# Attention with decay and a two-layer FFN on one core: in the second sweep, the FFN's second layer by seven block products instead of eight

## The chip, the cores and the metric

The kernel runs on one core of one Trainium2 chip. The metric is the time of one execution in microseconds (us): the median of three runs is 1243.39 us, from 1242.62 to 1245.14. The engines are named as in the profile: PE multiplies matrices (PEld loads its weights), DVE, ACT and POOL do elementwise work, SP's queue issues the transfers. PSUM is the memory that PE writes, in eight banks of 128 x 512 fp32; SBUF is the memory that everything else works in.

## The reference, cut to what matters

```python
# q, k, v: (8, 8, 576, 64), f: (8, 8, 576); x: attention's output as (8, 576, 512)
def _moe_ref(x, U, V, w_ch1, w_ch2):
    xt = x.transpose(0, 2, 1)
    h = xt @ U @ V
    u = x + h.transpose(0, 2, 1)
    ch = np.maximum(u @ w_ch1, 0.0) @ w_ch2      # 512 -> 2048 -> 512
    return (u + ch).astype(np.float32)
```

Ahead of it stands a causal attention whose scores are shifted by cumulative sums of log f. The hidden layer has 2048 channels: 16 chunks of 128.

## The kernel before, in words

All is fp32. A matmul operand is held as two tiles, a high part (rounded for the matmul) and a low part (the rest), and a product is three matmuls: high by high, low by high, high by low.

**First sweep** (up to about 752 us). Batch by batch it computes attention, u, and the FFN over hidden chunks 0 to 5. It writes to DRAM u transposed, in two parts (`ud`), and u plus the FFN so far (`accd`). Near its end it decodes the weights of chunks 6 to 15, which arrive as 64-bit words, on DVE (`wb_unit`, with tile `xn2` as scratch).

**Second sweep** (line 950 to the end) computes chunks 6 to 15 for nine groups of 512 token rows: the main rows of the eight batches and one group of all their tails. `order` is batch 7, 0, 1, ..., 5, the tails, 6. I count groups from 1.

- Group 1 goes chunk by chunk: `first` (12 matmuls into a bank), `relu`, `second`.
- Groups 2 to 9 go by pairs of chunks, five to a group, in `pair_of_chunks`. The **first layer** of a pair is already done by Strassen's scheme (in Winograd's form): seven products M1 to M7, each of 6 matmuls of 256 columns (`product`, L1069). It needs sums of weight blocks (`weight_sums`, made once) and sums of token blocks: `token_sums`, eight POOL additions of 128 x 512 at the third pair of the group before (L1052 to L1057), and `token_part`, which splits the four sums into `Th` and `Tl` in the last pair. DVE adds the products up from PSUM, seven additions of 128 x 256 a pair (`plus`, L1092). ACT takes the ReLU (L970), and DVE makes the low part by SCALAR_TENSOR_TENSOR, STT from here on (L971), from SBUF alone.
- The **second layer** of a pair (`second`, L993) is 24 matmuls of 512 columns into four banks `O`, one for each 128 token rows, which collect over all five pairs. They are done one pair later, dealt out between the products (the list `ready`). After the fifth pair DVE adds each bank to the rows of `accd` (L997), and SP stores them (L999).

PE's order is the program's (`manual_schedule`); the other queues are ordered by the scheduler. The products of the first layer take turns in four banks, two of pool `psF` and two of `psX`. `load_u` (L962) brings both parts of the next group's tokens into one of two buffers, 2 MB a whole group ahead. `xn0` and `xn1` hold the rows of `accd` in turn, `xn2` the sums of tokens.

Of the kernel before, what the change touches and what calls it, by code (L numbers as in the profile page):

```python
# [40 lines left out]
def tile_decay_attention_moe(ctx, tc, qk, v, f, U, V, w1, w2, out):  # L41
# [917 lines left out]
    def load_u(g):  # L959
        t = up.tile([P, 2, NDC, MAIN], F32R, tag="u", name=f"u{g}")  # L960
        for x in range(2):
            nc.sync.dma_start(t.bitcast(F32)[:, x], ud[g, :, x])  # L962
# [4 lines left out]

    def relu(h, src, cols):
        hh, hl = h[0][:, cols], h[1][:, cols]
        nc.scalar.activation(hh, src, AF.Relu)  # L970
        nc.vector.scalar_tensor_tensor(hl, src, 0.0, hh.bitcast(F32), op0=ALU.max, op1=ALU.subtract)  # L971
# [12 lines left out]

    def second(z, i, h, x):

        k = z["done"][x]
        z["done"][x] += 1
        if k == 0:
            z["po"][x] = psO.tile([P, DM], F32, tag="O", name=f"O{z['g']}_{x}")  # L990
        po = z["po"][x]
        for m, (ht, wt_) in enumerate(((h[0], b2h), (h[1], b2h), (h[0], b2l))):
            nc.tensor.matmul(po, ht[:, P * x : P * x + P], wt_[i], start=k == 0 and m == 0, stop=k == NB - 1 and m == 2)  # L993
        if k < NB - 1:
            return
        g, o = z["g"], z["acc"][:, x]
        nc.vector.tensor_tensor(o, po, o, op=ALU.add)  # L997
        if g < B:
            nc.sync.dma_start(out[g, P * x : P * x + P], o)  # L999
# [9 lines left out]
    for i in range(NB // 2):  # L1009
# [9 lines left out]
    Th = sf.tile([P, 4, 2, HT], F32R, tag="uh", name="Th")  # L1019
    Tl = sf.tile([P, 4, 2, HT], F32R, tag="ul", name="Tl")  # L1020
    tmp = [sf2.tile([P, 2, HT], F32, tag="ost", name=f"sum{x}") for x in range(2)]
    tmp.append(sf.tile([P, 2, HT], F32, tag="TS", name="sum2"))
    tmp = [t[:, y] for t in tmp for y in range(2)]
# [21 lines left out]
    whole_u = xn[2][:, 0:4].rearrange("p q (c t) -> p q c t", c=2)  # L1045

    def token_sums(u):

        for q in range(4):
            c, t = 2 * (q // 2), HT * (q % 2)  # L1050
            h, l = (x[:, c : c + 2, t : t + HT].bitcast(F32) for x in u)
            nc.gpsimd.tensor_tensor(whole_u[:, q], h, l, op=ALU.add)  # L1052
# [8 lines left out]

    T1, T3, T4, T2 = ([x[:, q] for x in (Th, Tl)] for q in range(4))

    def product(bank, tag, name, a, b):
        ps = bank.tile([P, 512], F32, tag=tag, name=name)[:, 0:HT]
        m = 0
        for c in range(2):
            for x, y in ((0, 0), (1, 0), (0, 1)):
# [1 line left out]
                m += 1  # L1070
        return ps

    def pair_of_chunks(z, u, i, ready, renew):

        def go(k):
            for fn in ready[:k]:
                fn()
            del ready[:k]  # L1080
# [4 lines left out]
        def f(k, a, b):
            return product(psF, "F", f"M{k}_{g}_{i}", a, b)

        def x(k, a, b):
            return product(psX, "X", f"M{k}_{g}_{i}", a, b)

        def plus(dst, ps, other):
            nc.vector.tensor_tensor(dst, ps, other, op=ALU.add)  # L1092
# [7 lines left out]
        nc.scalar.copy(s1, m1)  # L1100
# [28 lines left out]

    order = [B - 1, *range(B - 2), B, B - 2]  # L1130
    u = cur
    ready = []
    with tc.manual_schedule(engines={ET.PE}):
        for n, g in enumerate(order):
            un = load_u(order[n + 1]) if n + 1 < NG else None
            acc = xn[(n + 1) % 2]
            if n:
                nc.sync.dma_start(acc[:, 0:NM], accd[g].rearrange("x p d -> p x d"))
            z = {"g": g, "acc": acc, "po": [None] * NM, "done": [0] * NM}
            if n == 0:  # L1140
                for i in range(NB):
                    h = first(g, u, i)
                    for fn in ready:
                        fn()
                    ready = [lambda z=z, x=x, i=i, h=h: second(z, i, h, x) for x in range(NM)]
                    if i % 2 and i < 6:
                        weight_sums(i // 2)
                    if i == NB - 3:
                        token_sums(un)
                for q in (3, 0, 1, 2):  # L1150
                    token_part(q)
            else:
                for i in range(NB // 2):
                    pair_of_chunks(z, u, i, ready, un and i == NB // 2 - 1)
                    if n == 1 and i < 2:
                        spare = xn[2].rearrange("p c d -> p (c d)")
                        weight_sums(3 + i, [spare[:, 256 * y : 256 * y + 256] for y in range(5)])
                    if i == 2 and un:
                        token_sums(un)
            u = un  # L1160
# [50 lines left out]
```

## Time and profile before

| | |
|---|---|
| median of three runs | 1243.39 us |
| the profiled execution: its time, its span | 1242.59 us, 1240.8 us |
| PE busy | 1204.0 us (97%) |
| DVE, ACT, POOL busy | 861.3, 645.5, 424.5 us |
| from 861.55 to 914.34 us (five pairs): PE, DVE, ACT, POOL busy | 52.79, 27.53, 12.42, 15.91 us |

The span runs from the first instruction to the last; the time has 1.8 us around it. A row of groups gives line, engine, operation, tiles, shapes and count, then busy time and the mean of one in ns, then the engine's idle time before them and who ended it. A matmul's duration includes its way through the array, so two that follow each other overlap: the pace of PE is read from starts. In the rows of a timeline, the first two numbers are start and duration in us, and the brackets at the end hold the idle time before and who ended it. PE's clock (PEclk) is a share of full speed.

### The profile page before, as it was taken

Reading aid. Unit: us, or ns where it says so; the run is one execution under the profiler, and the core shown is the slowest. Engines: PE = TensorE matmul, PEld = TensorE weight load, DVE = VectorE, ACT = ScalarE, POOL = GpSimd, SP = SyncE. Lnnn points to the kernel's source line nnn. Section 1 sums busy time; section 2 is a strip of 40 time slices with the busy share of each in tenths; the row PEclk is TensorE's granted clock in tenths of the full one; section 3 lists DMA queues with packets and bytes.
Section 4 is the critical chain, followed back from the end, with each engine's and each line's share of the span. In section 5 each row is a group of like instructions: output and inputs, shape, how many; then the busy total and the mean of one; then the engine's idle time right before and its main releaser. Section 6 shows DMA issues by size and latency. Waiting matters only on the chain.

```text
span 1240.8 us, 21851 instructions
## 1 busy us (share of the span) xinstructions
PE 1204.0 (97%) x7824; PEld 1066.0 (86%) x7824; DVE 861.3 (69%) x2195; ACT 645.5 (52%) x1741; POOL 424.5 (34%) x377
## 2 busy tenths in 40 slices
PE   8998999999999999999999999989999999999998
PEld 5776898998989988989989888878988889888897
DVE  8877778768778778787686799684554645546443
ACT  5777678767778758777675444322122221212211
POOL 4223454534544435454541000441341413315100
PEclk9999999999999999999999999999999999999999
DMA  6544344525335325425342345121120312213010
GB/s 183 153 132 130 79 105 111 151 68 159 95 89 164 88 78 148 117 71 171 79 125 76 120 141 229 34 69 69 68 102 35 136 43 95 85 52 137 1 35 35
DMA packets 67581, 125.87 MB, mean 101 GB/s; under 512 B 7408, under 2 KB 31984, under 8 KB 65424
## 3 DMA queue, kind: packets, MB, share of 16 engines
q1 hardware_dynamic: 67408, 124.47, 32.8%
q8 instruction: 62, 1.02, 0.3%
q14 instruction: 47, 0.39, 0.1%
q10 hardware_dynamic: 64, 0.00, 0.0%
HBM read 88.65 MB, written 35.78 MB: 100 GB/s over the span
## 4 chain that ended last, share of the span: by engine, by line
PE 82%; DVE 8%; ACT 6%; issue 2%; DMA 2%; SPq 0%; ACTq 0%; POOL 0%; DVEq 0%; POOLq 0%
PE O L993 20%; PE M L1069 16%; PE A L700 10%; PE B L718 9%; PE V L543 5%; PE T L440 3%; PE S L344 3%; PE Hb L979 2%; PE V L515 2%; PE S L345 2%; ACT P L373 1%; ACT G L309 1%; PE Tt L609 1%; PE St L344 1%; PE S L341 1%
## 5 line engine op out<-in xcount | busy, mean ns | idle before, releaser
L1092 DVE TENSOR_TENSOR sum<-M,sum 128x256 f32<-128x256 f32 x280 | 117.7, 422 | 173.3 <-PE M L1069 172.3
L970 ACT ACTIVATE bh<-sum 128x256 fp32r<-128x256 f32 x160 | 66.3, 418 | 256.9 <-DVE sum L1092 256.8
L373 ACT ACTIVATE P<-S,nm 128x128 f32<-128x128 f32 (+3 forms) x256 | 137.5, 539 | 57.5 <-DVE nm L365 48.3
L365 DVE CUSTOM_DVE_ANT_0 S<-S,mask 128x128 f32<-128x128 f32 (+3 forms) x256 | 125.7, 495 | 53.5 <-PE S L345 46.8
L993 PE MATMUL O<-b2h,bh 128*128 128x512 f32 x360 | 143.0, 397 | 0.0
L993 PE MATMUL O<-b2l,bh 128*128 128x512 f32 x360 | 142.4, 396 | 0.0
L993 PE MATMUL O<-b2h,bl 128*128 128x512 f32 x360 | 141.8, 394 | 0.0
L700 PE MATMUL A<-uh,w1h 128*128 128x256 f32 (+1 forms) x384 | 120.3, 313 | 1.8 <-DVE hl L704 1.7
L309 POOL CAST G<-qk 64x576 fp32r<-64x576 f32 x52 | 34.9, 671 | 250.1 <-PE St L345 149.5
L700 PE MATMUL A<-ul,w1h 128*128 128x256 f32 (+1 forms) x384 | 113.5, 296 | 0.0
L700 PE MATMUL A<-uh,w1l 128*128 128x256 f32 (+1 forms) x384 | 113.5, 296 | 0.0
L185 POOL TENSOR_TENSOR Tl<-xn,Th 128x512 fp32r<-128x512 f32 x32 | 41.3, 1303 | 201.7 <-PE M L1069 178.1
L971 DVE SCALAR_TENSOR_TENSOR bl<-sum,bh 128x256 fp32r<-128x256 f32 x160 | 92.4, 581 | 19.4 <-ACT bh L970 19.0
L1052 POOL TENSOR_TENSOR xn<-u 128x512 f32<-128x512 f32 x32 | 43.7, 1391 | 167.6 <-DVE b1l L71 106.4
L718 PE MATMUL B<-w2h,hh 128*128 128x512 f32 x216 | 90.4, 418 | 2.3 <-DVE hl L704 1.3
L440 PE MATMUL T<-ident,P 128*128 128x128 f32 x544 | 85.5, 273 | 0.0
L718 PE MATMUL B<-w2l,hh 128*128 128x512 f32 x216 | 85.1, 394 | 0.0
L718 PE MATMUL B<-w2h,hl 128*128 128x512 f32 x216 | 84.6, 392 | 0.0
L422 DVE TENSOR_TENSOR PTl<-T,PTh 128x512 fp32r<-128x512 f32 (+1 forms) x156 | 79.0, 524 | 6.6 <-ACT PTh L419 6.3
L993 PEld LDWEIGHTS O<-b2l,bh 128*128 128x128 f32 x360 | 67.7, 188 | 16.5
L322 POOL TENSOR_TENSOR G<-qk,G 64x576 fp32r<-64x576 f32 x52 | 74.4, 1431 | 15.6 <-ACT G L309 6.2
L993 PEld LDWEIGHTS O<-b2h,bl 128*128 128x128 f32 x360 | 68.2, 189 | 11.2
(240 smaller groups left out, 3543.7 us busy)
## 6 DMA issues: line engine op xcount, KB each, us to landing
qk<-in_qk_dram SPq DMA_DIRECT2D x104, 288.0 KB
u<-ud SPq DMA_DIRECT2D x16, 1024.0 KB
sr<-in_w_dram SPq DMA_DIRECT2D x20, 512.0 KB
vr<-in_v_dram SPq DMA_DIRECT2D x32, 256.0 KB
accd<-ost SPq DMA_DIRECT2D x32, 256.0 KB
xn<-accd SPq DMA_DIRECT2D x8, 1024.0 KB
out_dram<-xn SPq DMA_DIRECT2D x32, 256.0 KB
ud<-uh SPq DMA_DIRECT2D x7, 1024.0 KB
```

Source lines behind the costliest of these rows:

```text
L322: pin(el.tensor_tensor(g[oth, 2, cols], k[oth], gf[oth, 2, cols], op=ALU.subtract))
L365: nc.vector.tensor_tensor_reduce(ps[:, :w], ps[:, :w], mask[:, 512 - w : 512], scale=-SCALE, scalar=3.0e38, op0=ALU.add, op1=ALU.min, accu ...
L373: nc.scalar.activation(pt, ps[:, :w], AF.Exp, bias=z["nm"][:, col : col + 1], scale=-1.0, accum_out=z["sm"][:, col : col + 1])
L422: defer(2, lambda: nc.vector.tensor_tensor(dstl, src, dsth.bitcast(F32), op=ALU.subtract))
L440: nc.tensor.transpose(tp[:, P * x : P * x + P], z["P"][j][i][:, P * c : P * c + P], ident)
L700: nc.tensor.matmul(ps[:, :nt], wt[:, fc, c], ut[:, c, sl], start=m == 0, stop=m == 3 * NDC - 1)
L718: nc.tensor.matmul(ps, ht[:, fc, P * x : P * x + P], wt[:, fc], start=fc == 0 and m == 0, stop=fc == NA - 1 and m == 2,)
L970: nc.scalar.activation(hh, src, AF.Relu)
L971: nc.vector.scalar_tensor_tensor(hl, src, 0.0, hh.bitcast(F32), op0=ALU.max, op1=ALU.subtract)
L993: nc.tensor.matmul(po, ht[:, P * x : P * x + P], wt_[i], start=k == 0 and m == 0, stop=k == NB - 1 and m == 2)
L1069: nc.tensor.matmul(ps, a[x][:, c], b[y][:, c], start=m == 0, stop=m == 5)
L1092: nc.vector.tensor_tensor(dst, ps, other, op=ALU.add)
```

## The change

From group 3 on, the second layer of a pair is also done by Strassen's scheme. The pair's hidden block (256 channels x 512 tokens) is cut into four quarters and the weights likewise. Seven products N1 to N7, each of 6 matmuls of 256 columns, take the place of 24 matmuls of 512. In group 2 (`plain_products`) the second layer stays as it was, since its weight sums are made during that group.

- **Banks.** N1, N3, N4, N5 (`psM`) and N6, N7 (`psF`) each collect over the five pairs in a bank of their own. That leaves two banks (`psX`) for M1 to M7 and for N2, which is not collected in PSUM: DVE adds it to the output rows in each pair. Eight products a pair go through two banks in turn.
- **Hidden sums.** Three of the seven hidden operands are quarters after the ReLU (X11, X12, X22), as before. Four are sums of quarters (S1 to S4): a ReLU on ACT, four STTs on DVE, each of which needs the one before (L1243 to L1246), and four splits with the high part on ACT and the low part on POOL (L185). Before, the fourth quarter had its STT alone: three STTs more a pair on DVE, 20 to 35 a group.
- **End of a group.** Seven wide additions on DVE and one copy on ACT in place of four additions on DVE, and three additions on POOL (L1107), after which the rows are stored.
- **Weights.** `weight_sums2`: eight POOL, four DVE and four ACT instructions for each of five pairs, during group 1, group 2 and the start of group 3.
- **Tokens.** The buffers of `load_u` are gone. `load_direct` brings the three blocks that are used as they are, again for each group during its predecessor's last pair. `load_whole` brings the high part into `xn2` and the low part into that one of `xn0` and `xn1` that held the output of the group before. So the low part (1 MB) is loaded only when those rows have been stored.

The diff, cut to its core:

```diff
-    up = pool("up", 2)
-    hp_ = pool("hp", 4)
-    psO = ctx.enter_context(tc.tile_pool(name="psO", bufs=4, space=PSUM, reuse_waits="tile"))
+    two = pool("two")
+    psM = ctx.enter_context(tc.tile_pool(name="psM", bufs=1, space=PSUM, reuse_waits="tile"))
     psX = ctx.enter_context(tc.tile_pool(name="psX", bufs=2, space=PSUM, reuse_waits="tile"))
...
+    def load_whole(g, x, home):
+        nc.sync.dma_start(home[:, 0:NM], ud[g, :, x])
...
+    def weight_sums2(i):
+        eng = nc.gpsimd
...
+        whole(t0, 0, 1)
+        whole(t1, 0, 0)
+        whole(t2, 1, 1)
+        whole(t3, 1, 0)
+        nc.vector.tensor_tensor(t1, t0, t1, op=ALU.subtract)
...
+        for src, (h, l) in zip((t1, t0, t2, t3), [block2(i, 0, 1)] + SD[i]):
+            split(h, l, src, nc.scalar, eng)
...
-            nc.gpsimd.tensor_tensor(whole_u[:, q], h, l, op=ALU.add)
+            nc.gpsimd.tensor_tensor(whole_u[q], whole_u[q], low[:, c : c + 2, t : t + HT], op=ALU.add)
...
+        def ends_6():
+            add(u4, z["M"][6], u4)
+            add(u3, z["M"][7], u4)
+            add(u4, z["M"][5], u4)
+            for q in (2, 3):
+                add(quarter[q], u3, quarter[q], nc.gpsimd)
+            for x in (2, 3):
+                store(z["g"], acc, x)
+
+        def ends_3():
+            add(quarter[1], z["M"][3], quarter[1])
+            add(quarter[1], u4, quarter[1], nc.gpsimd)
+            for x in (0, 1):
+                store(z["g"], acc, x)
...
+        work = (
+            (1, X11, block2(i, 0, 0)), (4, X22, sd[2]), (2, X12, block2(i, 1, 0)), (7, S3, sd[0]),
+            (5, S1, block2(i, 0, 1)), (6, S2, sd[1]), (3, S4, block2(i, 1, 1)),
+        )
...
+        m3 = pr(3, W4, D3)
+        add(c12, m3, s4)
+        slot(3)
+        if plain:
+            relu(*S3, c12)
+            ready.extend(plain_products(z, i))
+            return
+        nc.scalar.activation(r21, c12, AF.Relu)
+        nc.vector.scalar_tensor_tensor(c22, c22, 0.0, r21, op0=ALU.max, op1=ALU.add)
+        nc.vector.scalar_tensor_tensor(r21, c11, 0.0, r21, op0=ALU.max, op1=ALU.subtract)
+        nc.vector.scalar_tensor_tensor(c11, c11, 0.0, c22, op0=ALU.max, op1=ALU.subtract)
+        nc.vector.scalar_tensor_tensor(c21, c21, 0.0, c11, op0=ALU.max, op1=ALU.add)
+        for src, (h, l) in ((r21, S3), (c22, S1), (c11, S2), (c21, S4)):
+            split(h, l, src, nc.scalar, nc.gpsimd)
+        ready.extend(output_products(z, i))
...
+                if i == 1 and nxt is not None:
+                    load_whole(nxt, 0, xn[2])
+                    load_whole(nxt, 1, other)
+                if i == 2 and nxt is not None:
+                    token_sums(other)
```

PE's order in a pair is now M1, N1, M6, N4, M5, N2, M2, N7, M7, N5, M4, N6, M3, N3, where the N belong to the pair before.

On DVE, before, at the border of the second and third pair of group 5 (batch 3; `M3_3_1` is M3 of batch 3, pair 1, counted from 0): the addition of M3, two STTs of which neither needs the other, and the additions of the next pair.

```order
L1092 TENSOR_TENSOR sum1_9781<-M3_3_1_11829,sum1_9781 128x256
L971 SCALAR_TENSOR_TENSOR bl3_3_11753<-sum1_9781,bh3_3_11752 128x256
L971 SCALAR_TENSOR_TENSOR bl3_2_11751<-sum1_9781,bh3_2_11750 128x256
L1092 TENSOR_TENSOR sum0_9780<-M6_3_2_11859,sum0_9780 128x256
L1092 TENSOR_TENSOR sum1_9781<-M5_3_2_11867,sum0_9780 128x256
L1092 TENSOR_TENSOR sum2_9782<-M2_3_2_11884,sum0_9780 128x256
```

At the same place now: `xn0`, `xn1` and `xn2` here are spare rows of those tiles that hold the temporaries, and `N2_3_1` is the product that is added to the output in SBUF.

```order
L1107 TENSOR_TENSOR xn0_105<-M3_3_1_12200,xn0_105 128x256
L1243 SCALAR_TENSOR_TENSOR xn1_106<-xn1_106 128x256
L1244 SCALAR_TENSOR_TENSOR xn1_106<-xn0_105,xn1_106 128x256
L1245 SCALAR_TENSOR_TENSOR xn0_105<-xn0_105,xn1_106 128x256
L1246 SCALAR_TENSOR_TENSOR xn2_107<-xn2_107,xn0_105 128x256
L1107 TENSOR_TENSOR sum2_9782<-M6_3_2_12244,sum2_9782 128x256
L1107 TENSOR_TENSOR xn0_105<-M5_3_2_12258,sum2_9782 128x256
L1107 TENSOR_TENSOR xn1_106<-N2_3_1_12266,xn1_106 128x2x256
L1107 TENSOR_TENSOR xn0_105<-M2_3_2_12274,sum2_9782 128x256
```

The chain of four STTs, behind a ReLU, now stands ahead of the addition that empties M6's bank, and the wide addition of N2 stands between those of M5 and M2.

On POOL, before, the whole work of a group (`u4` is the next batch's tokens):

```order
L1052 TENSOR_TENSOR xn2_107<-u4_11645 128x512 x4
L1054 TENSOR_TENSOR xn2_107<-xn2_107 128x512
L1055 TENSOR_TENSOR xn2_107<-xn2_107 128x512
L1056 TENSOR_TENSOR xn2_107<-xn2_107 128x512
L1057 TENSOR_TENSOR xn2_107<-xn2_107 128x512
L185 TENSOR_TENSOR Tl_9779<-xn2_107,Th_9778 128x512 x4
```

Now, from the end of a group to the token sums of the next but one: the three output additions, mixed with the four low parts of the first pair (`hb`, in the order S1, S3, S2, S4), then the token sums, mixed with those of the second pair.

```order
L1107 TENSOR_TENSOR xn0_105<-sum0_9780,xn0_105 128x2x256 x2
L185 TENSOR_TENSOR hb_9771<-xn1_106,hb_9771 128x256
L1107 TENSOR_TENSOR xn0_105<-sum1_9781,xn0_105 128x2x256
L185 TENSOR_TENSOR hb_9771<-xn1_106,hb_9771 128x256
L185 TENSOR_TENSOR hb_9771<-xn0_105,hb_9771 128x256
L185 TENSOR_TENSOR hb_9771<-sum2_9782,hb_9771 128x256
L1085 TENSOR_TENSOR xn2_107<-xn2_107,xn0_105 128x2x256 x3
L185 TENSOR_TENSOR hb_9771<-xn1_106,hb_9771 128x256
L1085 TENSOR_TENSOR xn2_107<-xn2_107,xn0_105 128x2x256
L185 TENSOR_TENSOR hb_9771<-xn1_106,hb_9771 128x256
```

S3 of the second pair, the last row, which N7 waits for, now stands behind all four L1085, and these read the low part of the tokens (`xn0`) that is loaded over the stored output.

More of the change, by code (lines that the diff above doesn't have):

```diff
@@ L980, in first, with store @@
                 m += 1
-        h = hidden(f"{g}_{i}")
-        relu(h, ps, slice(0, MAIN))
-        return h
[L985 to L997, printed above, removed]
+        flat = hb.rearrange("p k x t -> p (k x t)")[:, 2 * MAIN * (i % 3) : 2 * MAIN * (i % 3) + 2 * MAIN]
+        h = flat[:, 0:MAIN], flat[:, MAIN : 2 * MAIN]
+        relu(*h, ps)
+        return h
+    def store(g, acc, x):
+        o = acc[:, x]
         if g < B:
@@ L1002, in second @@
             nc.sync.dma_start(out[2 * x, MAIN:S], o[64:128])
+    def second(z, i, h, x):
+        if i == 0:
+            z["po"][x] = psM.tile([P, DM], F32, tag=BANKS[x], name=f"O{z['g']}_{x}")
+        po = z["po"][x]
+        for m, (ht, wt_) in enumerate(((h[0], b2h), (h[1], b2h), (h[0], b2l))):
+            nc.tensor.matmul(po, ht[:, P * x : P * x + P], wt_[i], start=i == 0 and m == 0, stop=i == NB - 1 and m == 2)
+        if i < NB - 1:
+            return
+        o = z["acc"][:, x]
+        nc.vector.tensor_tensor(o, po, o, op=ALU.add)
+        store(z["g"], z["acc"], x)
     n3 = 3 * 2 * P
@@ L1008, in tile_decay_attention_moe @@
     SW = []
-    for i in range(NB // 2):
+    for i in range(NK):
         blocks = []
@@ L1018, in tile_decay_attention_moe, with block2 @@
         SW.append(blocks)
[L1019 to L1023, printed above, removed]
+    wide = 4 * 2 * HT
+    turned = [sf.tile([P, wide + 2 * HD], F32R, tag=tag, name=name) for tag, name in (("uh", "Th"), ("ul", "Tl"))]
+    Th, Tl = (t[:, 0:wide].rearrange("p (q c t) -> p q c t", q=4, c=2) for t in turned)
+    places = [sw2[:, HD * y : HD * y + HD] for y in range(6 * NK - 4)]
+    places += [t[:, wide + HD * y : wide + HD * y + HD] for t in turned for y in range(2)]
+    SD = [[places[6 * i + 2 * x : 6 * i + 2 * x + 2] for x in range(3)] for i in range(NK)]
+    wides = [sf2.tile([P, 2 * HT], F32, tag="ost", name=f"sum{x}") for x in range(2)]
+    ends = sf.tile([P, 2 * HT], F32, tag="TS", name="sum2")
+    tmp = [t[:, HT * y : HT * y + HT] for t in [ends] + [x[:, NM] for x in xn] for y in range(2)]
     def block(i, r, c):
         return [w[2 * i + r][:, 2 * c : 2 * c + 2] for w in (b1h, b1l)]
+    def block2(i, r, c):
+        return [w[2 * i + r][:, HD * c : HD * c + HD] for w in (b2h, b2l)]
     def weight_sums(i, tmp=tmp):
@@ new lines, in plain_products, with one @@
+    def plain_products(z, i):
+        acc = z["acc"]
+        def one(x, r, h):
+            if i == 0 and r == x // 2:
+                z["M"][x] = psM.tile([P, DM], F32, tag=BANKS[x], name=f"O{z['g']}_{x}")
+            ps = z["M"][x]
+            for m, (p_, wt_) in enumerate(((0, b2h), (1, b2h), (0, b2l))):
+                nc.tensor.matmul(
+                    ps, h[p_][:, P * (x % 2) : P * (x % 2) + P], wt_[2 * i + r],
+                    start=i == 0 and r == x // 2 and m == 0, stop=i == NK - 1 and r != x // 2 and m == 2,
+                )
+            if i == NK - 1 and r != x // 2:
+                add(acc[:, x], ps, acc[:, x])
+                store(z["g"], acc, x)
+        work = [(x, r, h) for r, h, xs in ((0, X11, (0, 1)), (1, X22, (2, 3)), (1, X12, (0, 1)), (0, S3, (2, 3))) for x in xs]
+        return [lambda y=y: one(*y) for y in work]
@@ L1130, in tile_decay_attention_moe @@
     order = [B - 1, *range(B - 2), B, B - 2]
-    u = cur
+    turns = [0]
     ready = []
     with tc.manual_schedule(engines={ET.PE}):
[L1134 to L1160, printed above, removed]
@@ new lines, in tile_decay_attention_moe @@
+        z = {"g": order[0], "acc": xn[1], "po": [None] * NM}
+        load_whole(order[1], 0, xn[2])
+        load_whole(order[1], 1, xn[0])
+        for k in range(3):
+            load_direct(order[1], k)
+        for i in range(NB):
+            h = first(order[0], cur, i)
+            for fn in ready:
+                fn()
+            ready = [lambda z=z, x=x, i=i, h=h: second(z, i, h, x) for x in range(NM)]
+            if i % 2 and i < 6:
+                weight_sums(i // 2)
+            if i == NB - 4:
+                token_sums(xn[0])
```

187 lines of the change are left out of this document (125 added, 62 removed).

## Prediction

> **What bounds the kernel now.** I read the page first, then the table by stages, the chain of waits, and the timelines of single engines.
>
> ```profile
> PE 1204.0 (97%) x7824; PEld 1066.0 (86%) x7824; DVE 861.3 (69%) x2195; ACT 645.5 (52%) x1741; POOL 424.5 (34%) x377
> PE 82%; DVE 8%; ACT 6%; issue 2%; DMA 2%; SPq 0%; ACTq 0%; POOL 0%; DVEq 0%; POOLq 0%
> ```
>
> PE is busy for 97% of the span and carries 82% of the chain that ended last. In the part that changes it is more than that. The table by stages gives, for group 4 and for ten microseconds of group 2, PE, PEld, DVE, ACT and POOL busy, then the granted clock:
>
> ```profile
> 861.55:914.34 52.79, 52.79 (x331) 47.41 (x331) 27.53 (x60) 12.42 (x29) 15.91 (x13) 1.00 0.22 79
> 815.00:825.00 10.00, 7.41 (x41) 6.65 (x41) 9.94 (x27) 3.63 (x10) 1.29 (x1) 0.83 0.43 140
> ```
>
> From group 3 on PE never stops and has its full clock, and the others are half idle: whatever PE is spared counts in full, as long as nobody makes it wait. In group 2 it does wait, for DVE, which is full there (9.94 of 10.00).
>
> **PE's own work.** The chain gives PE's pace, and ACT's copy of M1, one per pair, the length of a pair.
>
> ```profile
> 1083.63 2.13 PE M L1069 x18
> 1106.86 2.11 PE O L993 x9
> 915.39 0.37 ACT L1100 COPY sum<-M 128x256 f32<-128x256 f32 x1 [1.29 <-PE M L1069]
> 925.94 0.38 ACT L1100 COPY sum<-M 128x256 f32<-128x256 f32 x1 [1.27 <-PE M L1069]
> ```
>
> A matmul of 256 columns takes 2.13/18 = 0.118 us, one of 512 takes 2.11/9 = 0.234. A pair now: 42 x 0.118 + 24 x 0.234 = 10.6; measured 52.79/5 = 10.56, and 10.55 between the copies. Afterwards it is 84 matmuls of 256 columns: 84 x 0.1183 = 9.94, and a product of six 0.71. Groups 3 to 9 have 35 pairs: 35 x 0.62 = **21.7 us less**. Group 2 keeps its matmuls.
>
> **DVE's chain.** What the new scheme asks of DVE is shown by these groups (count, then busy time and mean in ns): first a quiet stretch, then one in which POOL runs without a break. After them single instructions, and ACT's ReLU over the whole sweep.
>
> ```profile
> L1092 DVE TENSOR_TENSOR sum<-M,sum 128x256 f32<-128x256 f32 x8 | 3.4, 424 | 7.1 <-PE M L1069 7.1
> L971 DVE SCALAR_TENSOR_TENSOR bl<-sum,bh 128x256 fp32r<-128x256 f32 x4 | 1.7, 420 | 0.6 <-ACT bh L970 0.6
> ...
> L971 DVE SCALAR_TENSOR_TENSOR bl<-sum,bh 128x256 fp32r<-128x256 f32 x3 | 2.6, 872 | 0.0
> L1092 DVE TENSOR_TENSOR sum<-M,sum 128x256 f32<-128x256 f32 x3 | 1.2, 416 | 0.2 <-PE M L1069 0.2
> ...
> 924.14 1.27 DVE L971 SCALAR_TENSOR_TENSOR bl<-sum,bh 128x256 fp32r<-128x256 f32 x1
> 1000.34 0.28 PE L1069 MATMUL M<-Th,b1h 128*128 128x256 f32 x1
> 1000.61 0.42 DVE L1092 TENSOR_TENSOR sum<-M,sum 128x256 f32<-128x256 f32 x1 [1.54 <-PE M L1069]
> ...
> L970 ACT ACTIVATE bh<-sum 128x256 fp32r<-128x256 f32 x160 | 66.3, 418 | 256.9 <-DVE sum L1092 256.8
> ```
>
> An STT reads twice from SBUF: 0.42 us alone, 0.87 on average and up to 1.27 beside POOL. The sum, which reads PSUM once, stays at 0.42. It starts 0.27 after its product's end (the next product's first matmul starts at 1000.34). The Trainium skill, page "SBUF — State Buffer", section "Who interferes with whom", says that a DVE instruction with two SBUF inputs contends with a GpSimd (here POOL) instruction that reads SBUF, and one with a single SBUF input does not. On who contends the trace agrees; what that section says of how much is a rival, below.
>
> In a pair's order M3 ends at 13 x 0.71 = 9.24, that is 0.71 before the next pair. Counted from that pair's start: sum of M3 from -0.44 to -0.02, ReLU to 0.40, then four STTs each needing the one before, and only then the sum that empties M6's bank. N2 takes that bank and is due at 5 x 0.71 = 3.55. With 0.42 each the chain ends at 2.1 and the sum, held then by M6 itself, at 2.8: hidden. With 0.87 it ends at 3.9, the sum at 4.3: PE waits 0.75. With 1.27: 5.5, 5.9, PE waits 2.4. So the price of a chain hangs on what POOL does beside it.
>
> **POOL's queue at a group's start.** Its prices, over the sweep or an earlier stretch, with the load that the token sums wait for and the last stores:
>
> ```profile
> L1052 POOL TENSOR_TENSOR xn<-u 128x512 f32<-128x512 f32 x24 | 32.4, 1379 | 41.4 <-DMA u<-ud 41.4
> L185 POOL TENSOR_TENSOR Tl<-xn,Th 128x512 fp32r<-128x512 f32 x25 | 32.2, 1297 | 180.2 <-PE M L1069 159.6 <-ACT Th L182 20.6
> ...
> L185 POOL TENSOR_TENSOR VS<-vr,VS 128x640 fp32r<-128x640 f32 x26 | 40.7, 1566 | 25.8 <-ACT VS L182 24.0 <-DMA qk<-in_qk_dram 1.8
> L595 POOL TENSOR_TENSOR xl<-xn,xh 128x512 fp32r<-128x512 f32 x31 | 40.5, 1308 | 2.4
> ...
> 913.25 0.80 SPq L962 DMA_DIRECT2D u<-ud  x2
> 1235.81 2.43 SPq L999 DMA_DIRECT2D out_dram<-xn  x4
> ...
> 921.13 5.43 POOL L1052 TENSOR_TENSOR xn<-u 128x512 f32<-128x512 f32 x4 [6.67 <-DMA u<-ud]
> ...
> L997 DVE TENSOR_TENSOR xn<-O,xn 128x512 f32<-128x512 f32 x3 | 2.0, 682 | 0.3 <-PE O L993 0.3
> ```
>
> A low part of 256 columns isn't in the trace: half of 1.30 is 0.65; by 1308 against 1566 ns for 128 columns more it is 1308 - 2 x 258 = 0.79. I take 0.75. A store lands at most 1240.8 - (1235.81 + 2.43) = 2.6 after its issue; I take 2.0. Two MB took 921.13 - 913.25 = 7.9, so 1 MB 3.9 at least and 7.9 at most; I take 4.5, near the half.
>
> Now the low token part is loaded over rows that must first be added up and stored. From a group's start: M3 of its first pair ends at 9.24 with N6 before it, the sums of the end (0.27 + 0.42 + 0.68) carry to 10.65, two POOL additions to 13.25, S1 to 14.0, the third addition to 15.3. Store landed 17.4, low part landed 22.0. Then POOL does three L1085 to 26.0, S1 of the second pair to 26.75, the fourth L1085 to 28.1, S3 to 28.85. N7 in the third pair needs S3 and is due at 2 x 9.94 + 7 x 0.71 = 24.85. **PE waits 4.0.** With 1.0 for the store and 3.9 for the load it is 2.4; with a load of 7.9 it is over 7.
>
> POOL is in use until about 35.5, beyond the third pair's chain: 0.75 to 2.4 more, I take 1.5, the middle. Chains of the first pair (output additions) and the last (token parts) have POOL beside them for half their length: 0.45 each. That of the second pair falls into POOL's wait for the load, that of the fourth meets only its own low parts: nothing. Per group 4.0 + 1.5 + 0.9 = 6.4.
>
> - Groups 4 to 8: 5 x 6.4 = 32.
> - Group 3: its predecessor is stored by DVE's additions at the end of the first pair, so S3 is in time. 1.5 + 0.9 for the chains, and 1.6, between nothing and 2.4, for the last `weight_sums2` beside the first of them: 4.
> - Group 9 has no token work: 0.45 beside the output additions, and 0.5, between nothing and 0.75, for each of four chains beside low parts alone: 2.5.
>
> Together **+38.5**, from +10 (every chain hidden, N7's wait halved) to +55 (STTs at 1.27).
>
> **Group 2's start.** Rows of POOL, PE and ACT there:
>
> ```profile
> 794.50 2.92 POOL L1052 TENSOR_TENSOR xn<-u 128x512 f32<-128x512 f32 x2 [5.37 <-DVE b2l L71]
> ...
> 806.06 0.28 PE L1069 MATMUL M<-u,b1h 128*128 128x256 f32 x1
> ...
> 806.97 0.37 ACT L1100 COPY sum<-M 128x256 f32<-128x256 f32 x1 [1.02 <-PE M L1069]
> 815.91 0.37 ACT L1100 COPY sum<-M 128x256 f32<-128x256 f32 x1
> 830.85 0.37 ACT L1100 COPY sum<-M 128x256 f32<-128x256 f32 x1 [0.69 <-PE M L1069]
> ...
> 818.41 0.38 PE L1069 MATMUL M<-Th,swhh 128*128 128x256 f32 x1 [2.59 <-DVE sum L1092]
> ```
>
> Before, tokens lie in a buffer of their own; only the sum into `xn2` waits for the weights' decoding, whose scratch that is (794.50). Now the load of `xn2` itself waits for it: 794.5 + 4 = 798.5, four L1085 at 1.38 to 804, then four subtractions and, of the token parts, three, at 1.30 to 813.1. M6 needs the part `T2` and is due at 806.06 + 0.71 + 6 x 0.234 = 808.2: PE waits 4.9. If `weight_sums2` of pair 0, now in group 1, delays the decoding by 4, it is 9. Before, the second pair took 14.9 by the copies, 4.4 over 10.56, by its stall and the clock; `weight_sums` still fills DVE, now behind a first wait, and I let it cost 5.5: 4.9 + 5.5 - 4.4 = **+6**, from +3 (half of it falls together with the new wait) to +12.
>
> The rest of group 2 gets four `weight_sums2`: 32 POOL instructions of 0.75, 16 STT-like ones on DVE with two SBUF inputs (0.42 to 1.27, 7 to 20 us) beside sums that PE waits for: **+4**, from 0 to +8.
>
> **The end.** The last matmuls and DVE's additions behind them:
>
> ```profile
> 1230.15 7.02 PE O L993 x30
> 1235.09 2.79 DVE L997 TENSOR_TENSOR xn<-O,xn 128x512 f32<-128x512 f32 x4 [3.57 <-PE O L993]
> ```
>
> After the last pair, 30 matmuls of 7.02 become 42 of 256 columns, 4.97: that is in the 0.62. But from M3's end on, S1's STT ends at 1.95, its high part at 2.4, its low part at 3.1, S3's at 3.9, and N7 is due behind N3, N1, N4 and N2, at 2.84: a wait of 1.0. And behind the last DVE addition POOL's (1.30) now stands ahead of the store: **+2.3**, from 1 to 3.5.
>
> **The sum.** The profiled execution took 1242.6 (span 1240.8 and 1.8 around it), near the median, 1243.4. -21.7 + 38.5 + 6 + 4 + 2.3 = +29.1: **1272**.
>
> **The rivals.**
>
> - *The waits are hidden.* A store of 1.0, a load of 3.9, four L1085 at 1.30 (-0.3) and low parts of 0.65 (-0.2): N7 waits 2.0; every chain hides: -21.7 + 10 + 4 + 1 + 2 = -4.7, about 1238. For it: DVE has 27.53 of 52.79 in use, and seven products of cover per chain. Against it: S3 is behind four L1085 in POOL's queue whatever its speed. It decides once N7's wait and the chains together come to less than (21.7 - 7)/5 = 2.9 a group instead of 6.4. Chance 0.22.
> - *The gain is just eaten:* N7 waits 2.4 and the chains take 0.1 a group; 12.5, and 9 elsewhere, against 21.7: no change. Chance 0.06.
> - *STTs at 1.27 throughout and the clock falls.* N7 4.0, the clock behind it 1.7, the third pair's chain 2.4, two half-covered ones 0.55 each: 9.2 a group; 5 x 9.2 + 6 + 3 = 55, group 2 +10 and +6, end +3: -21.7 + 74 = +52, about 1295. For it: POOL's work doubles, from 15.91 to 20 x 0.75 + 12 x 1.3 + 3 x 1.3 = 34.5 a group. In 815 to 825 a wait of 2.59 stood beside a clock of 0.83, that is 10 x 0.17 = 1.7 lost; N7's wait is longer. Against: the mean beside POOL was 0.87. Chance 0.22. The Trainium skill, page "TensorE: Matmul & The Clock Gate", section "Why this matters for your kernels", warns of idle gaps of PE over some 3 us; the row with 2.59 agrees roughly.
> - *DVE and POOL exclude each other.* An STT would wait for a whole POOL instruction, 1.30 + 0.42 = 1.72: third pair's chain at 7.3, PE waits 4.2 instead of 1.5, in six groups +16: 1288. Against: 1.27 is the longest shown. Chance 0.05. The Trainium skill, page "SBUF — State Buffer", section "Who interferes with whom", calls the shared pair of ports an exclusive lock, by which 1.72 would be seen; the 1.27 speaks against it.
>
> That the change does something else can be left out: PE's order has the 84 matmuls.
>
> **How the numbers follow.** Forecast 1272 (own range 1255 to 1287): 0.45. A measurement can tell some 0.2% (2.5 us). Faster 0.22, same 0.06, slower 0.45 + 0.22 + 0.05 = 0.72. The range takes in most of the first and third rival: 1236 to 1297.
>
> **What would show it.** Copies of M1 9.94 apart in undisturbed pairs; in the third pair of groups 4 to 8 a wait of PE of about 4 ahead of N7, released by POOL; waits of 1 to 2 ahead of N2, released by DVE; M6 of group 2 held about 5. I am wrong if N7 waits under 2, or if chains beside POOL stay near 0.42 an STT.

## The result and the profile after

The changed kernel takes 1295.08 us (median of four runs, 1292.88 to 1295.25) against 1243.97: a ratio of 1.0407, 95% interval 1.0389 to 1.0425. The direction held: slower was forecast. The time lies in the wide range, 1236 to 1297, which takes in most of two rivals, but outside the forecast's own, 1255 to 1287: 29 us were forecast and 51 measured. From the page of the profile after, PE's line and the chain:

```profile
PE 1209.7 (94%) x8454; PEld 1098.5 (85%) x8454; DVE 974.7 (75%) x2376; ACT 708.7 (55%) x1908; POOL 593.3 (46%) x578
PE 64%; DVE 15%; ACT 7%; POOL 6%; issue 4%; DMA 4%; POOLq 0%; SPq 0%; ACTq 0%; DVEq 0%
```

PE's share of the chain fell from 82% to 64%; DVE, POOL and DMA took it over. Where the time went is read from the copies of M1, whose distance is the length of a pair. First those at which groups 3 and 9 begin, of the kernel before, then of the changed one:

```profile
862.56 0.37 ACT L1100 COPY sum<-M 128x256 f32<-128x256 f32 x1 [1.29 <-PE M L1069]
1179.52 0.37 ACT L1100 COPY sum<-M 128x256 f32<-128x256 f32 x1 [1.29 <-PE M L1069]
```

```profile
874.67 0.35 ACT L1214 COPY sum<-M 128x256 f32<-128x256 f32 x1
...
1046.81 0.36 ACT L1214 COPY sum<-M 128x256 f32<-128x256 f32 x1
1057.81 0.37 ACT L1214 COPY sum<-M 128x256 f32<-128x256 f32 x1 [0.27 <-PE M L1102]
1069.53 0.37 ACT L1214 COPY sum<-M 128x256 f32<-128x256 f32 x1 [0.49 <-PE M L1102]
1084.61 0.37 ACT L1214 COPY sum<-M 128x256 f32<-128x256 f32 x1 [0.49 <-PE M L1102]
1094.64 0.37 ACT L1214 COPY sum<-M 128x256 f32<-128x256 f32 x1 [0.49 <-PE M L1102]
1105.01 0.35 ACT L1214 COPY sum<-M 128x256 f32<-128x256 f32 x1
...
1224.25 0.35 ACT L1214 COPY sum<-M 128x256 f32<-128x256 f32 x1
```

Up to group 3 the change loses 874.67 - 862.56 = 12.1 us. Groups 3 to 8 take 349.6 instead of 317.0, 32.6 more; group 9 and the end, with spans of 1291.1 and 1240.8, 66.9 instead of 61.3, 5.6 more: 50.3 in all.

The rows from 1046.81 to 1105.01 are group 6. Its pairs take 11.00, 11.72, 15.08, 10.03 and 10.37, where the matmuls alone take 9.94. PE's own rows in that group show who held it (the number before the arrow is PE's idle time):

```profile
1050.15 0.51 PE L1125 MATMUL N<-b2h,hb 128*128 128x256 f32 x2 [0.86 <-DVE xn L1107]
1061.09 0.50 PE L1125 MATMUL N<-b2h,hb 128*128 128x256 f32 x2 [0.46 <-DVE sum L1107]
...
1063.63 0.62 PE L1125 MATMUL N<-sw,hb 128*128 128x256 f32 x3 [0.59 <-POOL hb L185]
...
1077.20 0.86 PE L1125 MATMUL N<-sw,hb 128*128 128x256 f32 x5 [3.23 <-POOL hb L185]
```

The first two are N2, waiting for DVE in the first and second pair; the other two are N7, waiting for S3's low part, in the second pair and, for 3.23, in the third. What POOL did before that, and the low part's load on SP:

```profile
1070.79 3.78 POOL L1085 TENSOR_TENSOR xn<-xn,xn 128x512 f32<-128x512 f32 x3 [5.81 <-DMA xn<-ud]
1074.52 0.72 POOL L185 TENSOR_TENSOR hb<-xn,hb 128x256 fp32r<-128x256 f32 x1
1075.20 1.26 POOL L1085 TENSOR_TENSOR xn<-xn,xn 128x512 f32<-128x512 f32 x1
1076.42 1.42 POOL L185 TENSOR_TENSOR hb<-xn,hb 128x256 fp32r<-128x256 f32 x2
...
1065.49 0.33 SPq L972 DMA_DIRECT2D xn<-ud  x1
```

POOL idles 5.81 for the load (issued 1065.49, used 1070.79), then adds three blocks, S1's low part, the fourth block, and only then S3's. That is the chain that the prediction wrote out. What its sum did not count stands in the table of group 6 by stages (PE, PEld, DVE, ACT, POOL busy, granted clock):

```profile
1046.81:1105.01 58.20, 53.05 (x422) 51.95 (x422) 40.91 (x82) 20.18 (x51) 34.83 (x35) 0.97 0.29 100
1073.00:1077.20 4.20, 0.97 (x9) 0.76 (x8) 0.69 (x1) 0.00 (x0) 4.20 (x6) 1.00 0.00 0
1077.20:1084.00 6.80, 6.80 (x44) 6.80 (x45) 4.20 (x8) 1.54 (x4) 6.57 (x6) 0.75 0.42 154
```

Behind the wait PE runs for 6.80 us at 0.75 of its clock: 1.7 lost again.

### The profile page after: what moved, and what is told of

The parts are those of the page before. It is cut to its first block, busy times and chain, and to the rows that moved or that the text cites. A ratio compares the mean times of both kernels' runs of the same rounds, so it can differ in the third digit from the quotient of the medians.

```text
span 1291.1 us, 24113 instructions
## 1 busy us (share of the span) xinstructions
PE 1209.7 (94%) x8454; PEld 1098.5 (85%) x8454; DVE 974.7 (75%) x2376; ACT 708.7 (55%) x1908; POOL 593.3 (46%) x578
## 4 chain that ended last, share of the span: by engine, by line
PE 64%; DVE 15%; ACT 7%; POOL 6%; issue 4%; DMA 4%; POOLq 0%; SPq 0%; ACTq 0%; DVEq 0%
PE A L700 9%; PE B L718 9%; PE M L1102 9%; PE N L1125 9%; PE V L543 5%; PE T L440 3%; PE S L344 2%; POOL xn L1085 2%; PE V L515 2%; PE S L345 2%; DVE xn L1107 2%; DVE hb L976 2%; POOL hb L185 2%; DMA xn<-ud 2%; PE S L341 1%
## 5 line engine op out<-in xcount | busy, mean ns | idle before, releaser
L185 POOL TENSOR_TENSOR hb<-xn,hb 128x256 fp32r<-128x256 f32 x122 | 95.4, 806 | 95.3 <-ACT hb L182 95.3
L975 ACT ACTIVATE hb<-xn 128x256 fp32r<-128x256 f32 x105 | 43.9, 418 | 168.4 <-DVE xn L1107 168.4
L1125 PE MATMUL N<-b2h,hb 128*128 128x256 f32 x560 | 110.3, 289 | 11.4 <-DVE sum L1107 7.0
L1125 PE MATMUL N<-sw,hb 128*128 128x256 f32 x546 | 86.4, 292 | 21.9 <-POOL hb L185 21.9
L1125 PEld LDWEIGHTS N<-b2h,hb 128*128 128x128 f32 x560 | 87.9, 193 | 14.7 <-DVE sum L1107 8.6
L1125 PEld LDWEIGHTS N<-sw,hb 128*128 128x128 f32 x546 | 75.5, 198 | 24.5 <-POOL hb L185 24.4
L976 DVE SCALAR_TENSOR_TENSOR hb<-xn,hb 128x256 fp32r<-128x256 f32 x105 | 65.3, 631 | 26.2 <-ACT hb L975 26.2
L1085 POOL TENSOR_TENSOR xn<-xn,xn 128x512 f32<-128x512 f32 x32 | 41.7, 1328 | 89.2 <-DMA xn<-ud 89.2
L322 POOL TENSOR_TENSOR G<-qk,G 64x576 fp32r<-64x576 f32 x52 | 74.6, 1434 | 15.6 <-ACT G L309 6.2
L1125 PE MATMUL N<-b2l,hb 128*128 128x256 f32 x280 | 80.2, 286 | 0.0
L323 POOL TENSOR_TENSOR G<-qk,G 64x576 fp32r<-64x576 f32 x52 | 74.9, 1441 | 5.1 <-ACT G L309 4.9
```

The costliest lines, as they stand in the source:

```text
L185: leng.tensor_tensor(dl, src, dh.bitcast(F32), op=ALU.subtract)
L322: pin(el.tensor_tensor(g[oth, 2, cols], k[oth], gf[oth, 2, cols], op=ALU.subtract))
L323: pin(em.tensor_tensor(g[own, 1, cols], q[own], gf[own, 0, cols], op=ALU.subtract))
L976: nc.vector.scalar_tensor_tensor(l, src, 0.0, h.bitcast(F32), op0=ALU.max, op1=ALU.subtract)
L1125: nc.tensor.matmul(ps[:, y], a[p_][:, P * y : P * y + P], w[q_], start=(i == 0 or k == 2) and y == 0 and m == 0, stop=(i == NK - 1 or k == ...
```

## The experiments

The theory: POOL's queue holds S3 behind token sums that wait for the load, and the clock falls behind that wait. The rival: POOL simply has too much to do, and where it runs, DVE's chain of STTs is slow.

### e1: no load for POOL to wait for

```diff
                     load_whole(nxt, 0, xn[2])
-                    load_whole(nxt, 1, other)
```

> The load of the low token part is left out from group 2 on (the token sums add the old rows in its place), so that POOL no longer waits for store and load; its work is the same. Now the third pairs of groups 4 to 8 take 14.1 to 16.7 us instead of 9.94, 28 in sum. Theory (N7's wait on S3, behind token sums that wait for the load, and the lower clock behind that wait): all five come down to about 10, the time to 1267. Rival (POOL has too much work, and beside it DVE's chain is too slow): the token sums now stand beside the chains of the first two pairs, most of the 28 comes back there, 1280 or more.

Measured: 1285.70, ratio 1.0322 (1.0303 to 1.0340). The copies of group 6:

```profile
1048.60 0.36 ACT L1214 COPY sum<-M 128x256 f32<-128x256 f32 x1
1059.60 0.37 ACT L1214 COPY sum<-M 128x256 f32<-128x256 f32 x1 [0.27 <-PE M L1102]
1074.36 0.35 ACT L1214 COPY sum<-M 128x256 f32<-128x256 f32 x1
1084.67 0.37 ACT L1214 COPY sum<-M 128x256 f32<-128x256 f32 x1 [0.48 <-PE M L1102]
...
1068.57 0.42 DVE L1107 TENSOR_TENSOR xn<-M,sum 128x256 f32<-128x256 f32 x1 [3.20 <-POOL hb L185]
...
1066.65 0.86 PE L1125 MATMUL N<-sw,hb 128*128 128x256 f32 x5 [1.27 <-POOL hb L185]
```

The third pair is down from 15.08 to 10.31, so the load was what held it. But the second is up from 11.72 to 14.76: the token sums now mix with the first pair's low parts. PE waits 1.27 for S3's low part (the last row) and, in pieces of up to 0.5, for DVE, which itself waits 3.20 for a low part before it may overwrite its source. The theory's mechanism held, its number (1267) did not; the rival's number did.

### e2: POOL in the order of the program

```diff
-    with tc.manual_schedule(engines={ET.PE}):
+    with tc.manual_schedule(engines={ET.PE, ET.Pool}):
```

> POOL works in the order of the program: the token sums behind the low parts of the second pair and the third, all else of the change as it is; load and store stay. Theory: S3 of the second pair no longer waits for the load, third pairs of groups 4 to 8 at 10 to 11; the third output addition now stands ahead of S1 and S3 of the first pair, up to 1 more in each second pair; 1267 to 1273. Rival (POOL's amount of work, not its order): token sums run beside the third and fourth chain and Tl comes late, 1285 or more.

Measured: 1289.25, ratio 1.0350 (1.0334 to 1.0367). By the copies of M1, third pairs came to 10.1, but the last pairs of a group rose from 10.4 to between 14.0 and 15.6. PE, DVE and POOL at the start of such a last pair, in group 4:

```profile
981.24 0.80 PE L1125 MATMUL N<-b2h,hb 128*128 128x256 f32 x2 [2.94 <-DVE xn L1107]
...
976.63 1.40 DVE L1244 SCALAR_TENSOR_TENSOR xn<-xn,xn 128x256 f32<-128x256 f32 x1
978.07 1.38 DVE L1245 SCALAR_TENSOR_TENSOR xn<-xn,xn 128x256 f32<-128x256 f32 x1
979.48 1.37 DVE L1246 SCALAR_TENSOR_TENSOR sum<-sum,xn 128x256 f32<-128x256 f32 x1
980.77 0.41 DVE L1107 TENSOR_TENSOR xn<-M,sum 128x256 f32<-128x256 f32 x1
...
976.39 1.36 POOL L1088 TENSOR_TENSOR xn<-xn 128x512 f32<-128x512 f32 x1
977.83 1.33 POOL L1089 TENSOR_TENSOR xn<-xn 128x512 f32<-128x512 f32 x1
979.24 1.33 POOL L1090 TENSOR_TENSOR xn<-xn 128x512 f32<-128x512 f32 x1
...
981.20:987.00 5.80, 5.76 (x27) 5.77 (x28) 1.78 (x4) 1.63 (x4) 4.78 (x6) 0.50 0.30 97
```

The chain fell beside the last token sums. Each STT lasts as long as the POOL addition beside it, 1.4 instead of 0.42; the sum of M6 comes late, N2 waits 2.94, and the clock stands at 0.50 for 5.8 us (the last row, by stages). Again one wait was exchanged for another, and again the rival seemed to win.

### e3: everything but the products of the second layer

```diff
-pair_of_chunks(z, i, ready, renew if nxt is not None and i == NK - 1 else None, n == 1)
+pair_of_chunks(z, i, ready, renew if nxt is not None and i == NK - 1 else None, True)
```

From group 3 on it multiplies by weight blocks that `weight_sums2` has overwritten; the work is that of the plain products.

> All groups use plain_products: no chain, no hidden sums, no products N, 24 matmuls of 512 columns a pair as before; buffers, two banks for M1 to M7, loads and weight sums of the change stay. Theory (chain and N7 make the waits): groups 3 to 9 take 52.8 each again, only the 12 us of group 1 and 2 stay, 1256. Rival (two banks in place of four and the low load over the stored rows cost by themselves): groups 4 to 8 stay at 55 or more, 1270.

Measured: 1259.33, ratio 1.0113 (1.0095 to 1.0132). By the copies of M1, groups 3 to 8 take 52.2 to 52.9, as before the change. Two banks, the new loads and their order cost nothing as long as no chain and no N7 hang on them: what remains is the start of the sweep.

### e4: the wait on N7 filled with matmuls by zero

```diff
+            if k == 7 and i == 1 and 3 <= z["n"] <= 7:
+                for _ in range(26):
+                    nc.tensor.matmul(ps[:, 0], zero, w[0], start=False, stop=False)
```

> In the third pair of groups 4 to 8, 26 matmuls by a tile of zeros stand ahead of N7, 26 x 0.118 = 3.1 us, in N7's own bank; they fill the wait of 3.2 to 4.5. Theory (a gap of PE of that length is followed by a lower clock, which costs 1.4 to 2.9 again): the wait stays, the clock stays full behind it, 5 x 2 = 10 less, about 1285. Rival (the clock falls for another reason, or matmuls by zero do not count): 1295, or up to 10 more where N7 was ready earlier.

Measured: 1288.49, ratio 1.0352 (1.0329 to 1.0374). The filling in group 6, and the stage behind it:

```profile
1070.10 3.27 PE L1127 MATMUL N<-sw,zero 128*128 128x256 f32 x26
...
1074.00:1080.10 6.10, 6.10 (x54) 6.10 (x53) 4.33 (x8) 1.55 (x4) 5.87 (x6) 1.00 0.54 173
```

N7 starts no earlier, but the clock stays at 1.00 where it was 0.75. By the copies, the third pairs of groups 4 to 8 took 14.10, 16.09, 15.08, 16.72 and 16.15 and now 14.17, 14.18, 14.19, 14.33 and 14.18: 7.1 less, of 10 expected. In group 4 the clock had stayed full, and nothing was to be had.

### e5: POOL's order once more, with the token sums between the chains

To e2 is added, with `token_sums` cut in two (`token_adds` are the four L1085, `token_sums` the four subtractions):

```diff
                     load_whole(nxt, 1, other)
+                    token_adds(other)
                 if i == 2 and nxt is not None:
-                    token_sums(other)
+                    token_sums()
```

> As e2 (POOL in the program's order), and the eight token sums in two halves: four additions behind the low parts of the second pair, four subtractions behind those of the third, so that each half stands between two chains. In e2 the chain of the fourth pair ran beside four token sums with 1.4 us for each STT, N2 waited 2.9 and the last pair took 15.5 instead of 10.4. Theory (what costs is POOL beside the chain, not POOL's amount): the last pairs come to 10.4, the third pairs stay near 10, 6 x 5 = 30 less than e2, about 1259. Rival (POOL has too much to do, wherever it stands): the wait only moves to another pair, 1280 or more.

Measured: 1256.12, ratio 1.0099 (1.0071 to 1.0127). Group 5 by stages, and the chain of its fourth pair, which in e2 stood beside the last token sums:

```profile
975.41:1027.81 52.40, 50.75 (x417) 49.77 (x417) 40.47 (x82) 20.20 (x51) 35.26 (x35) 1.00 0.31 108
...
1017.94 0.56 DVE L1245 SCALAR_TENSOR_TENSOR xn<-xn 128x256 f32<-128x256 f32 x1 [0.55 <-ACT xn L1244]
1018.53 0.42 DVE L1246 SCALAR_TENSOR_TENSOR xn<-xn,xn 128x256 f32<-128x256 f32 x1
1018.99 0.42 DVE L1247 SCALAR_TENSOR_TENSOR xn<-xn,xn 128x256 f32<-128x256 f32 x1
1019.45 0.42 DVE L1248 SCALAR_TENSOR_TENSOR xn<-xn,xn 128x256 f32<-128x256 f32 x1
```

The group takes 52.40 instead of some 59, with POOL's 35 instructions and their 35 us unchanged, three STTs of this chain at 0.42 and the clock at 1.00. The rival falls: POOL does not have too much to do. It stood in the wrong places, ahead of S3 in the change itself, among low parts in e1, beside a chain in e2. This reordering alone takes 39 of the 51 back.

### e6 and e7: the start of group 2, and the additions at a group's end

e6 loads group 2's tokens into a free place early; e7 moves a group's last additions, here cut to two of them:

```diff
-        load_whole(order[1], 0, xn[2])
-        load_whole(order[1], 1, xn[0])
+        whole = sw2[:, n2 - 2 * NDC * MAIN : n2].bitcast(F32).rearrange("p (x c t) -> p x c t", x=2, c=NDC)
+        for x in range(2):
+            nc.sync.dma_start(whole[:, x], ud[order[1], :, x])
...
-            add(quarter[0], z["M"][1], quarter[0])
+            late[2] = lambda: add(quarter[0], z["M"][1], quarter[0])
...
+        def ends_3():
+            late[8] = rows_23
+            late[9] = rows_01
```

> As e5, and the tokens of group 2 are loaded early into the place of the second layer's weight sums, which aren't made yet, so that their loads do not wait for the decoding whose scratch is xn2. Theory (the load behind the decoding costs 4.9 to 9 at the first pair of group 2, which took 18.4 instead of 8.9): first pair of group 2 back to 9 to 11, 8 less than e5, 1251. Rival (DVE's weight sums hold that pair anyway): no more than 2 less.

> As e5, and the additions at a group's end moved: N1's behind the sum of M2, N4's and N5's behind those of M7 and M4, the last two and POOL's three behind the chain of the first pair. Theory (in first and second pairs of a group, 11.0 and 11.7 instead of 9.94, these additions stand ahead of the sum of M6 and beside the chain): about 10.3 each, 7 x 1.3 = 9 less than e5, 1250. Rival (the tokens' POOL work of the last pair and S3's way cost it): within 3 of e5; or worse, as the stores and with them the low load come 2 later.

Measured: e6 1253.67, ratio 1.0071 (1.0050 to 1.0091); e7 1254.78, ratio 1.0076 (1.0051 to 1.0101). e6's first pair of group 2 came from 17.35 to 14.47, not to 9 to 11: DVE's weight sums hold it next (PE waits 1.14 and 2.19 there for DVE, at 816.23 and 819.39). Its 2.4 less lies within what the runs scatter: those of e5 are up to 6.0 apart. In e7 the first two pairs fell as expected, from 10.6 and 11.4 to 10.0 and 10.5, but the fourth rose from 10.0 to 11.6: the stores and with them the low part came later, and the four additions fell beside the third pair's chain. It gains nothing, for the reason that its expectation ends with.

### e8: both, and DVE in the order of the program

```diff
-    with tc.manual_schedule(engines={ET.PE, ET.Pool}):
+    with tc.manual_schedule(engines={ET.PE, ET.Pool, ET.DVE}):
```

> e6 and e7 together, and DVE too in the order of the program. If both theories hold, 8 and 9 less than e5: 1242, at the time of before. If DVE's order of the program brings waits of its own: 1250 or more.

Measured: 1275.36, ratio 1.0239 (1.0209 to 1.0268). Waits of its own, then: one of PE of 7.65 in group 3, and second pairs of 12.3 from group 5 on. The first is DVE's order: from 891.95 DVE waits 4.03 for POOL's part of the last weight sums, then does its own four additions for them, and only at 899.43 the sum of M6 that N2 waits for. What makes the second pairs long stays open. The first pair of group 2 took 9.03, near the 8.94 of the kernel before, but the third took 16.35.

### e9 and e10: the low part in two halves, and all of it together

```diff
-                    load_whole(nxt, 1, other)
+                    for c in (2, 0):
+                        nc.sync.dma_start(other[:, c : c + 2], ud[nxt, :, 1, c : c + 2])
```

The four additions follow in the order of the halves. e10 adds to e9 the early load of e6 and one line: in the last group the third output addition is on DVE.

> As e7, and the low token part is loaded in two halves, that of the rows stored first ahead, and added in that order. In e7 first and second pairs came to 10.0 and 10.5, but the low part landed 2 later and its four additions stood beside the chain of the third pair (STTs of 1.4, N2 waits 1.8, fourth pair 11.6). Theory: the additions start 1 to 2 earlier, the fourth pair comes to 10 to 10.6, 5 x 1.2 = 6 less than e7, about 1248. Rival (stores in one queue hold both halves, as the last store waits for POOL): no more than 2 less.

> e9 with the early token load of e6, and in the last group one of the three output additions on DVE in place of POOL: 2 less for the first pair of group 2 and 1 less at the end, 1245 if e9 comes to 1248, which is the time of before. Rival (what PE gains is used up by what is left in group 2, at the ends of groups and at the end of the kernel): it stays over before by 0.2% or more.

Measured: e9 1243.80, ratio 0.9990 (0.9973 to 1.0007); e10 1237.08, ratio **0.9936** (0.9912 to 0.9961). Both came out below what was expected, 1248 and 1245: the fourth pairs of groups 4 to 8, 11.5 to 12.2 in e7, took no more than 10.0 in e9, as the theory has it. Five pairs of e10, the last of group 6 and four of group 7, by stages:

```profile
1060.77:1111.15 50.38, 50.38 (x422) 50.22 (x421) 39.00 (x83) 20.67 (x51) 35.63 (x36) 1.00 0.36 116
```

PE is busy in all of these 50.38 us, against 52.79 for five pairs before and 49.7 for the matmuls alone. So the gain of the new scheme is real, and it can be had with the same products: 2.4 of the 3.1 us a group. What e10 still loses against before stands, by the copies, ahead of group 2's first product (2.6 us), in group 2 (57.0 against 55.6), and in group 9 and the end (63.5 against 61.3); group 3 gains nothing yet (53.0 against 52.8).

## Why the prediction was right and where it fell short

| stage | predicted | measured |
|---|---|---|
| group 1 and 2 | +6 + 4 = +10 | +12.1 |
| groups 3 to 8 | 4 + 32 - 6 x 3.1 = +17.4 | +32.6 |
| group 9 and the end | 2.5 + 2.3 - 3.1 = +1.7 | +5.6 |

**Right: PE's gain.** e10 shows pairs of 50.38/5 = 10.1 where nothing holds PE, 0.1 over the 9.94.

**Right: N7 behind the token sums.** 4.0 was forecast; the third pairs of groups 4 to 8 show 3.19, 3.20, 3.23, 4.46 and 3.23, with POOL's rows in the order that the prediction used. e1 shows the load as the cause. That the size is so near is in part luck. In group 6, counted from its first product (1045.57), the load was issued at 19.9 (17.4 forecast) and N7 got S3's low part at 31.6 (28.85); but N7 itself was due at 28.1 instead of 24.85, because the first two pairs had lost 2.8.

**Wrong: the price of that wait.** "PE waits 4.0" was entered as 4.0. The fall of the clock behind a gap stood only in the third rival, not in the sum. In group 6 the third pair cost 15.08 - 9.94 = 5.1, and 4.2 to 6.8 in groups 4 to 8; e4 puts 7.1 us of the kernel on the clock alone. In the prediction itself stood the row with 2.59 beside 0.83, in the kernel before: with a forecast wait of 4.0 the clock belonged into the sum.

**Wrong: the chains of a group's first two pairs.** 0.45 each was forecast for the pairs behind the last and the first chain; 11.00 and 11.72 are 1.06 and 1.78 over. The prediction priced these chains by POOL's work beside them (token parts, output additions) and left out that the wide additions of the group's end stand in DVE's queue. In group 6 of the changed kernel, after the last chain:

```profile
1048.32 0.84 DVE L1246 SCALAR_TENSOR_TENSOR sum<-sum,xn 128x256 f32<-128x256 f32 x1
1049.09 0.68 DVE L1107 TENSOR_TENSOR xn<-N,xn 128x512 f32<-128x512 f32 x1
1049.69 0.41 DVE L1107 TENSOR_TENSOR xn<-M,sum 128x256 f32<-128x256 f32 x1
```

N1's addition (`N`, 0.68) is done ahead of the sum of M6 (0.41), which N2 waits for, and puts it off by 0.60; the last STT, 0.84 instead of 0.42 beside a low part on POOL, by 0.4, about the 0.45 that was forecast. In the second pair N2 waits 0.46 and N7 0.59, the latter for S3 behind POOL's third output addition. This wait follows from the prediction's own times: S3's low part at 15.3 + 0.75 = 16.05, N7 due at 9.94 + 4.97 = 14.91. It was left out.

With POOL in the program's order alone (e5) these pairs took 10.6 and 11.4; e7 and e9, which also move the group's last additions on DVE and on POOL, bring them to 10.0 and 10.5. How much of that is DVE's part and how much POOL's, no run separates.

**Wrong, the other way: the third pair's chain.** 1.5 was forecast; the fourth pair took 10.03, that is 0.1. N7's wait had held PE long enough for POOL to get past: in group 6 the last token sum ends at 1084.13, and the chain begins at 1084.16. In e2, without that wait, the same kind of chain cost 2.94 and the clock: it was a real price, but not one to be added to N7's.

**Wrong: the end.** The wait of 1.0 forecast for the last N7 came (1.05, at 1279.81). Behind the last product, one POOL addition of 1.30 was charged. The rows of POOL and SP there:

```profile
1283.63 3.70 POOL L1107 TENSOR_TENSOR xn<-sum,xn 128x512 f32<-128x512 f32 x3 [1.56 <-DVE sum L1107]
...
1286.14 2.06 SPq L994 DMA_DIRECT2D out_dram<-xn  x4
```

All three stand in a row behind the last sums on DVE, and the stores behind them: PE's last matmul ends at 1283.0, the span at 1291.1, 8.1 later; before it was 1240.8 - 1237.2 = 3.6. That is 4.5 more.

**Nearly right: the start.** T2 was to hold M6, group 2's second product, for 4.9. M6 waited for both its parts:

```profile
814.28 0.39 PE L1102 MATMUL M<-Th,swhh 128*128 128x256 f32 x1 [2.17 <-ACT Th L182]
817.66 0.58 PE L1102 MATMUL M<-Tl,swhh 128*128 128x256 f32 x1 [2.88 <-POOL Tl L185]
```

That is 5.05; by chance so near, as T2 came 4.6 later than forecast (817.66 instead of 813.1) and M6 was due 3.7 later. Behind the wait the clock stood at 0.60 from 817.6 to 823.6, 2.4 lost that no term held. By the copies group 2's first pair took 18.36 instead of 8.94, but its second 10.76 instead of 14.94: the 5.5 charged to the second did not come. Together these two pairs took 5.2 more where 6 was forecast, and the rest of the group 3.1 where 4 was.

The other 3.8 lie ahead of group 2's first product, at 810.74 by its copy instead of 806.97, and have no term in the prediction. Of these, 1.8 are two waits of PE for DVE in group 1 (1.09 at 758.27 and 0.72 at 762.29), while POOL works on `weight_sums2` of the first pair. They stand neither in the kernel before nor in e2 and e5, where POOL keeps the program's order and does these sums later. In the experiments this copy came between 807.34 and 814.26, so how much of the remaining 2 the change makes stays open.

The third rival gave the right total, 1295, and half of its mechanism: the clock fell, but from group 4 on no chain of STTs ran at 1.27 throughout, and the wide additions and the three POOL additions at the end are not in its sum. That its total fits is partly luck.

## What to carry to other kernels

An in-order queue is priced by its order: with the same 35 POOL instructions a group takes 59 or 52 us here, by where the waiting ones and the long ones stood against a chain on another engine. When a change gives an off-path engine more to do, write down for each pair what stands ahead of the one result that the critical engine needs, and move what waits for a transfer behind it before judging the change. Waits forecast for one place must be summed with what they trigger (here the clock) and not with what they hide (here the next chain).

## What the runs showed of the hardware

**STTs and POOL.** With POOL's additions of 128 x 512 back to back, an STT with two SBUF inputs took 1.37 to 1.40 us, as long as the POOL addition beside it, and both went on in step (e2); alone 0.42. The chain of group 3 in the changed kernel shows the same, ahead of the wait of 2.33 below:

```profile
897.44 1.40 DVE L1245 SCALAR_TENSOR_TENSOR xn<-xn,xn 128x256 f32<-128x256 f32 x1
```

The prediction took 0.87 on average, 1.27 at most. POOL's additions took 1.33 to 1.36 in e2 instead of 1.30, so nearly all of the delay is DVE's. The Trainium skill, page "SBUF — State Buffer", section "Who interferes with whom", calls the shared ports an exclusive lock, to which the prediction gave 0.05; the rows of e2 agree with it better than with an even split, though 1.40 is less than the full 1.72. That a lock is the mechanism is not shown by a run here.

**The clock.** In group 6 a gap of PE of 3.23 was followed by 6.8 us at 0.75, in e2 one of 2.94 by 5.8 at 0.50. Behind one of 2.33 in group 3 the changed kernel's clock was 0.73 as well, but behind one of 3.19 in group 4 it stayed full. Both gaps, and the stages behind them:

```profile
900.62 0.60 PE L1125 MATMUL N<-b2h,hb 128*128 128x256 f32 x2 [2.33 <-DVE sum L1107]
...
960.44 0.86 PE L1125 MATMUL N<-sw,hb 128*128 128x256 f32 x5 [3.19 <-POOL hb L185]
...
900.60:907.00 6.40, 6.38 (x40) 6.38 (x41) 3.24 (x6) 0.96 (x3) 6.11 (x7) 0.73 0.38 145
...
960.40:967.00 6.60, 6.56 (x55) 6.56 (x56) 4.33 (x8) 1.66 (x5) 6.36 (x6) 1.00 0.49 161
```

The Trainium skill, page "TensorE: Matmul & The Clock Gate", section "Why this matters for your kernels", puts the limit at about 3 us. Here it was no fixed length: 2.33 was enough once, 3.19 not enough another time, and what else decides it stays open. Matmuls by a tile of zeros kept the clock up (e4).
